# q and k transposed by VectorE in 32x32 blocks, with a new start and a new fill order, in an attention-then-MLP kernel

## The chip, the cores and the metric

One core of one Trainium2 chip. The metric is the device time of one execution in microseconds (us), as the median of several runs. A run is called fast when it lies within 1.5% of the fastest run of the same kernel.

## The reference, cut to what matters

For 8 batches of 8 heads, 576 tokens and 64 values per head, causal attention with a forget gate; its output, laid out as 4608 tokens by 512, goes through a two-layer MLP with an exact GELU.

```python
scores = scale * np.matmul(q, k.transpose(0, 1, 3, 2))
log_f = np.log(np.clip(f, 0.0001, 1.0)); cum = np.cumsum(log_f, axis=-1)
scores = np.where(causal, -1e9, scores + cum[..., :, None] - cum[..., None, :])
attn_out = softmax(scores) @ v                    # B, H, S, D
x = attn_out.transpose(0, 2, 1, 3).reshape(B * S, H * D)
h = x @ w_in                                      # 512 -> 2048
return (0.5 * h * (1 + erf(h / sqrt(2)))) @ w_out # 2048 -> 512
```

q and k are drawn at a scale of 0.1, so a score has a spread of about 0.01 x 8 / 8 = 0.01, and what the softmax does comes almost wholly from the decay.

## The kernel before

Heads go in pairs (four per batch). The score matmuls of this kernel take q and k with their 64 values on partitions; they are loaded with tokens on partitions, transposed by TensorE (PE) into PSUM, and copied by VectorE (DVE) to `qA`, `qB` (one head each, the other half zero) and `kT`:

```python
def transposes(b, i, which):                       # one head pair, q or k
    ps = o_psum.tile([P, 2, JT // 2, PT], BF16, tag="o", name="ps_t")
    for h in range(2):
        for j in range(JT // 2):
            nc.tensor.transpose(ps[:, h, j, :], src[:, 2*i+h, 2*j*D : 2*(j+1)*D], ident_bf[:PT, :PT])
    ...                                            # four copies of 64x288, PSUM -> qA/qB or kT
```

Per pair, `scores` makes four score tiles (PE), their exps (ScalarE, ACT) and causal masks (GpSimd, POOL); `attend` multiplies with v, which GpSimd has weighted by the gate (`weigh_v`). PE's idle moments in attention of batch b are filled with matmuls of `gemm2` of batch b - 1; after attention comes `gemm1`, among whose matmuls the transposes and `weigh_v` of the next batch lie:

```python
for b in range(B):
    fill = gemm2(b - 1) if b else iter(())
    load_qk(b + 2); load_v(b + 2)                  # two buffers each
    for i in range(HP):
        for t in range(4):
            scores(b, i, t)
            ...                                    # attend and normalize of pair i - 1
            take(fill, 2)
    ...                                            # last pair, rest of fill
    for ffb in range(n_ff):
        gemm1(b, ffb)
        if b + 1 < B:
            if ffb % 2 == 1: transposes(b + 1, ffb // 4, (ffb // 2) % 2)
            if ffb % 4 == 2: weigh_v(b + 1, ffb // 4)
```

In the traces every engine runs its instructions in the order in which the program issues them (in e3 below, eight load issues moved within GpSimd's order are worth 41 us). That order carries the whole argument.

The softmax here doesn't subtract the row's maximum and nothing guards it: scores larger than these inputs give would overflow.

## Time and profile before

| | before |
|---|---|
| time, median of 4 runs | 420.51 us (419.28 to 421.01) |
| gemm1 of batch 0 starts | 57.8 us |
| batch period, batches 2 to 6 | 42.8 us |
| gemm1 with transposes / attention, one batch | 15.9 / 26.8 us |
| VectorE per transposed batch | 32 copies of 0.48 us |

The period is the distance between the table loads for Exp on ScalarE, one at each start of attention (119.60 to 333.53 us for five batches). The prediction shows and reads the lines.

### The profile page before, as it was taken

To read this page: it belongs to the slowest core of one execution; us is meant where nothing else is said; L and a number is where in the kernel's file an instruction comes from. 1 tells how busy PE (TensorE), PEld (TensorE's weight loads), DVE (VectorE), ACT (ScalarE), POOL (GpSimd) and SP (SyncE) were. 2 spreads that over 40 slices of the span, in tenths; PEclk is the share of its full clock that TensorE was granted. 3 is DMA by queue.
4 is the path that set the end of the run, shared out by engine and by line. 5 is a ranking of instruction groups with operands and counts; after the bars stand their busy time and mean duration, and the time that the engine had idled before them with its cause. 6 is when DMAs were issued, how large, how long until landed. Compare 5 with 4: busy or idle time off the path is not lost.

```text
span 419.1 us, 7515 instructions
## 1 busy us (share of the span) xinstructions
PE 368.4 (88%) x3045; PEld 207.5 (50%) x3045; DVE 207.2 (49%) x466; ACT 215.0 (51%) x291; POOL 129.5 (31%) x262
## 2 busy tenths in 40 slices
PE   1340879899989998999899989998999999999996
PEld 1220645465546554655465546654664456444442
DVE  6930339534954486448634773468355924102001
ACT  3040736872677267725773577447743675350620
POOL 8408460446034603460247024700470042000000
PEclk9999969999999999999999999999999999999999
DMA  9999985801671166216521643100001000102002
GB/s 156 209 193 196 193 186 125 114 28 54 148 109 31 51 152 93 48 51 152 82 58 52 152 65 74 46 31 2 27 27 51 2 25 28 50 0 77 25 25 77
DMA packets 62738, 34.19 MB, mean 82 GB/s; under 512 B 43184, under 2 KB 57520, under 8 KB 62704
## 3 DMA queue, kind: packets, MB, share of 16 engines
q0 software_dynamic: 15328, 13.63, 20.9%
q1 hardware_dynamic: 47376, 20.08, 18.7%
q8 instruction: 24, 0.39, 0.4%
q14 instruction: 10, 0.08, 0.1%
HBM read 37.90 MB, written 9.44 MB: 113 GB/s over the span
## 4 chain that ended last, share of the span: by engine, by line
PE 77%; ACT 8%; POOL 5%; issue 4%; DVE 4%; ACTq 0%; POOLq 0%
PE ps L277 30%; PE ps L297 26%; PE s L210 7%; PE o L241 7%; ACT e L220 6%; PE ps_t L170 4%; POOL e L222 3%; PE ps_x L265 2%; DVE kT L181 2%; ACT L220 1%; DVE qB L181 1%; DVE qA L181 1%; POOL vw L195 1%; POOL q L98 1%; POOL k L98 1%
## 5 line engine op out<-in xcount | busy, mean ns | idle before, releaser
L289 ACT ACTIVATE g<-ps 128x512 bf16<-128x512 f32 x144 | 86.0, 597 | 125.7 <-PE ps L277 125.7
L297 PE MATMUL ps<-w_out_sb,g 128*128 128x512 bf16 x576 | 146.2, 379 | 0.0
L277 PE MATMUL ps<-xT_sb,w_in_sb 128*128 128x512 bf16 x576 | 136.5, 383 | 0.0
L220 ACT ACTIVATE e<-s 128x1024 bf16<-128x1024 f32 (+2 forms) x128 | 105.7, 862 | 56.2 <-PE s L210 47.6
L222 POOL TENSOR_SCALAR_AFFINE_SELECT e<-e 128x256 bf16<-128x256 bf16 x160 | 62.5, 406 | 114.7 <-ACT e L220 114.3
L277 PEld LDWEIGHTS <-w_in_sb 128*128 128x128 bf16 x576 | 54.0, 99 | 58.2 <-issue 3.5
L241 PE MATMUL o<-vw,e 128*128 128x65 bf16 x960 | 53.9, 196 | 17.7 <-POOL e L222 9.7
L297 PEld LDWEIGHTS <-g 128*128 128x128 bf16 x576 | 49.4, 98 | 37.8
L254 DVE RECIPROCAL r<-o 128x5 f32<-128x5 f32 x64 | 12.5, 195 | 110.5 <-PE o L241 110.5
L210 PE MATMUL s<-qA,kT 128*128 128x384 bf16 (+2 forms) x192 | 54.6, 289 | 11.3 <-ACT e L220 10.3
L181 DVE COPY kT<-ps_t 64x288 bf16<-64x288 bf16 x128 | 61.3, 479 | 2.5 <-PE ps_t L170 0.3
L306 DVE COPY ot<-ps 128x512 f32<-128x512 f32 x36 | 24.7, 687 | 75.7 <-PE ps L297 75.7
L210 PEld LDWEIGHTS <-kT 128*128 128x128 bf16 x384 | 37.2, 100 | 47.1 <-issue 17.2
L241 PEld LDWEIGHTS <-e 128*128 128x128 bf16 x960 | 45.5, 99 | 29.7 <-POOL e L222 11.3
L210 PE MATMUL s<-qB,kT 128*128 128x384 bf16 (+2 forms) x192 | 49.7, 290 | 0.0
L195 POOL TENSOR_TENSOR vw<-v,wT 128x640 bf16<-128x640 f32 x32 | 40.8, 1276 | 15.9 <-issue 13.1
L181 DVE COPY qA<-ps_t 64x288 bf16<-64x288 bf16 x64 | 30.6, 478 | 13.7 <-PE ps_t L170 12.5
L98 POOL DMA_DIRECT2D q<-in_q_dram x11 | 8.4, 766 | 80.3 <-PE ps_t L170 78.7
L255 DVE TENSOR_TENSOR x<-o,r 128x320 bf16<-128x320 f32 x64 | 31.4, 491 | 2.2
L181 DVE COPY qB<-ps_t 64x288 bf16<-64x288 bf16 x64 | 30.7, 480 | 0.9
L170 PE MATMUL ps_t<-ident_bf,q 96*128 96x96 bf16 x192 | 14.6, 216 | 11.6 <-POOL ident_bf masks.py:199 7.2
L170 PEld LDWEIGHTS <-q 96*128 96x128 bf16 x192 | 12.4, 103 | 18.9 <-issue 7.0
(33 smaller groups left out, 117.2 us busy)
## 6 DMA issues: line engine op xcount, KB each, us to landing
out_dram<-ot SPq DMA_DIRECT2D x36, 256.0 KB, 2.0
v<-in_v_dram SPq DMA_DIRECT2D x64, 128.0 KB, 3.1
q<-in_q_dram POOLq DMA_DIRECT2D x7, 576.0 KB, 6.0
k<-in_k_dram POOLq DMA_DIRECT2D x7, 576.0 KB, 8.0
w_in_sb<-in_moe_w_in_dram POOLq DMA_DIRECT2D x4, 512.0 KB, 12.1
v<-in_v_dram SPq DMA_DIRECT2D x8, 256.0 KB, 3.4
w_out_sb<-in_moe_w_out_dram POOLq DMA_DIRECT2D x4, 512.0 KB, 25.7
q<-in_q_dram POOLq DMA_DIRECT2D x4, 144.0 KB, 6.2
```

The source lines that it names most:

```text
L170: nc.tensor.transpose(ps[:, h, j, :], src[:, 2 * i + h, 2 * j * D : 2 * (j + 1) * D], ident_bf[:PT, :PT],)
L181: nc.vector.tensor_copy(rows[:, odd], ps[odd * D : (odd + 1) * D, h].rearrange("d j p -> d p j"),)
L195: nc.gpsimd.tensor_tensor(vw_of[b][:, hs, :, 0:D], v_of[b][:, hs, :, :], w.unsqueeze(3).to_broadcast([P, 2, NBLK, D]), Alu.mult,)
L210: nc.tensor.matmul(st[:, h, c : c + w], kT[i][:, K0[n] : K0[n] + P], qt[:, q0 : q0 + w], start=True, stop=True,)
L220: nc.scalar.activation(et[:, :, 0:c], st[:, :, 0:c], Act.Exp, scale=scale)
L222: nc.gpsimd.affine_select(out=et[:, :, c0 : c0 + P], in_=et[:, :, c0 : c0 + P], compare_op=Alu.is_ge, fill=0.0, base=0, pattern=[[0, 2], [ ...
L241: nc.tensor.matmul(o[:, m, :], e_of[b, i, t][:, h, c : c + P], vw_of[b][:, 2 * i + h, n, :], start=(n == 0), stop=(n == m),)
L255: nc.vector.tensor_tensor(x_of[b, i][:, :, h, :], o[:, :, 0:D], r.unsqueeze(2).to_broadcast([P, NBLK, D]), Alu.mult,)
L277: nc.tensor.matmul(ps, w_in_sb[:, kt, ffb * P : (ffb + 1) * P], xT_sb[:, kt, t0 : t0 + TC], start=(kt == 0), stop=(kt == n_dm - 1),)
L289: nc.scalar.activation(g_of[c][ffb], ps, Act.Gelu)
L297: nc.tensor.matmul(ps, g_of[c][kt][:, ts * P : (ts + 1) * P], w_out_sb[:, kt, :], start=(kt == 0), stop=(kt == n_ff - 1),)
L306: nc.vector.tensor_copy(ot, ps)
```

## The change

It is meant to take the 48 transposes per batch off PE, to start attention of batch 0 earlier, and to give PE filler work while ScalarE starts its exps. q and k of batches 2 to 7 are loaded twice, shifted by half a head, so that blocks of 32 columns can be transposed by VectorE in one instruction; a mask multiplication then separates the heads. The second layout is larger, and the pools of q, k and v shrink from two buffers to one (two of q and k would still have fitted, as e8 shows). The diff, cut to its core:

```diff
-    qk_pool = ctx.enter_context(tc.tile_pool(name="qk", bufs=2))
-    v_pool = ctx.enter_context(tc.tile_pool(name="v", bufs=2))
+    qk_pool = ctx.enter_context(tc.tile_pool(name="qk", bufs=1))
+    v_pool = ctx.enter_context(tc.tile_pool(name="v", bufs=1))
...
+    def load_qk_halves(b):                       # eight loads on GpSimd's queue
...
+        n = JD * D - D // 2
+                nc.gpsimd.dma_start(
+                    dst[:, i, 0:n],
+                    bass.AP(..., ap=[[D // 2, 2], [JD * D, 64], [1, n]]))
...
+    def transposes_dve(b, i, which):
+        src = qk_of[b][which][:, i, :].rearrange("p (j d) -> p j d", j=JD)   # JD = 18
+        dst = kT[i] if which else x_pool.tile([P, S], BF16, tag="qS", name="qS")
+        nc.vector.transpose(
+            dst.rearrange("d (p j) -> d j p", j=JD), src[:, :, 0 : D // 2]
+        )
+        if not which:
+            for h, qt in enumerate((qA[i], qB[i])):
+                nc.vector.tensor_scalar(qt, dst, hmask[:, h : h + 1], None, Alu.mult)
+
+    def transposes(b, i, which):
+        (transposes_pe if b == 1 else transposes_dve)(b, i, which)
...
+    FILL = [[0, 12, 4, 4], [2, 3, 3, 2], [2, 3, 3, 2], [2, 2, 2, 2], [8, 0, 4, 4]]
...                                               # batch 0 and 1: other start, loads reordered
     for b in range(B):
-        load_qk(b + 2)
-        load_v(b + 2)
+            load_v(b + 1)
+            attention(b, gemm2(b - 1), FILL_1 if b == 1 else FILL)
         for ffb in range(n_ff):
             gemm1(b, ffb)
             ...
+        load_qk_halves(b + 2)
```

Two details matter later. The view `"d (p j) -> d j p"` makes the transpose write one element of 2 bytes every 18 elements, that is every 36 bytes. And `load_qk_halves(b + 2)` stands on GpSimd's queue between `weigh_v` of batch b + 1 and the masks of batch b + 1, and can go only when batch b + 1 has been transposed out of the single buffer.

More of the change, by code (lines that the diff above doesn't have):

```diff
@@ L24 @@
 PT = 96
+JD = 18
 STILES = [
@@ L87, with load_qk_tokens @@
     qk_of, v_of = {}, {}
-    def load_qk(b, h0=0, h1=H):
-        if b >= B:
-            return
+    def load_qk_tokens(b, h0=0, h1=H):
         if b not in qk_of:
-            qk_of[b] = (
-                qk_pool.tile([PT, H, JT * D], BF16, tag="q", name=f"q{b}"),
-                qk_pool.tile([PT, H, JT * D], BF16, tag="k", name=f"k{b}"),
-            )
+            qk_of[b] = [
+                qk_pool.tile([P, HP * JD * D], BF16, tag=n, name=f"{n}{b}")[
+                    :PT, : H * JT * D
+                ].rearrange("p (h c) -> p h c", h=H)
+                for n in "qk"
+            ]
         for src, dst in zip((q, k), qk_of[b]):
@@ L101, in load_qk, with load_v @@
             )
-    def load_v(b, h0=0, h1=H):
+    def load_qk_halves(b):
         if b >= B:
             return
+        qk_of[b] = [
+            qk_pool.tile([P, HP * JD * D], BF16, tag=n, name=f"{n}{b}").rearrange(
+                "p (i c) -> p i c", i=HP
+            )
+            for n in "qk"
+        ]
+        n = JD * D - D // 2
+        for src, dst in zip((q, k), qk_of[b]):
+            for i in range(HP):
+                nc.gpsimd.dma_start(
+                    dst[:, i, 0:n],
+                    bass.AP(
+                        tensor=src.tensor,
+                        offset=src.offset + (b * H + 2 * i) * S * D,
+                        ap=[[D // 2, 2], [JD * D, 64], [1, n]],
+                    ),
+                )
+    def load_v(b, h0=0, h1=H, eng=None):
+        if b >= B:
+            return
+        eng = eng or nc.sync
         if b not in v_of:
@@ L108, in load_v @@
         vt = v_of[b]
+        eng.dma_start(
+            vt[:, h0:h1, 4, :], v[b, h0:h1, 448:S].rearrange("h p d -> p h d")
+        )
         for h in range(h0, h1):
-            nc.sync.dma_start(
+            eng.dma_start(
                 vt[:, h, 0:4, :],
@@ L113, in load_v @@
             )
-        nc.sync.dma_start(
-            vt[:, h0:h1, 4, :], v[b, h0:h1, 448:S].rearrange("h p d -> p h d")
-        )
     f_sb = consts.tile([BH, S], FP32)
     nc.sync.dma_start(f_sb, f.rearrange("b h s -> (b h) s"))
-    for i in range(HP):
-        load_qk(0, 2 * i, 2 * i + 2)
-    load_v(0)
+    load_qk_tokens(0, 0, 2)
     ident_bf = consts.tile([P, P], BF16)
@@ L128 @@
     make_identity(nc, ident_fp)
+    for i in range(1, HP):
+        load_qk_tokens(0, 2 * i, 2 * i + 2)
+    v_of[0] = v_pool.tile([P, H, NBLK, D], FP32, tag="v", name="v0")
+    nc.gpsimd.memset(v_of[0][:, :, 4, 0:1], 0.0)
+    load_v(0, 0, 4)
+    load_v(0, 4, 8)
     qA = [consts.tile([P, S], BF16, name=f"qA{i}") for i in range(HP)]
@@ L134 @@
         nc.vector.memset(qB[i][0:D, :], 0.0)
+    hmask = consts.tile([P, 2], FP32)
+    for r in range(4):
+        nc.vector.memset(hmask[32 * r : 32 * (r + 1), 0:1], float(r % 2 == 0))
+        nc.vector.memset(hmask[32 * r : 32 * (r + 1), 1:2], float(r % 2 == 1))
     w_in_sb = consts.tile([P, n_dm, d_ff], BF16)
@@ L141, with load_w_out @@
         nc.gpsimd.dma_start(w_in_sb[:, kt, :], w_in_r[:, kt, :])
-    load_qk(1)
-    load_v(1)
-    for kt in range(0, n_ff, 4):
-        nc.gpsimd.dma_start(w_out_sb[:, kt : kt + 4, :], w_out_r[:, kt : kt + 4, :])
+    def load_w_out():
+        for kt in range(0, n_ff, 4):
+            nc.gpsimd.dma_start(w_out_sb[:, kt : kt + 4, :], w_out_r[:, kt : kt + 4, :])
     wT = consts.tile([P, NBLK, BH], FP32)
@@ L158, with transposes_first, evac, transposes_pe @@
     nc.scalar.activation(wk, cum, Act.Exp, bias=cum[:, S // 2 : S // 2 + 1], scale=-1.0)
-    psw = o_psum.tile([P, NBLK, BH], FP32, tag="o", name="psw")
     xT_sb = consts.tile([P, n_dm, N_tok], BF16)
-    def transposes(b, i, which):
+    def transposes_first(i, which):
+        src = qk_of[0][which]
+        ps = o_psum.tile([P, JT, PT], BF16, tag="o", name="ps_f")
+        for h in range(2):
+            for j in range(JT):
+                nc.tensor.transpose(
+                    ps[h * D : (h + 1) * D, j, :],
+                    src[:, 2 * i + h, j * D : (j + 1) * D],
+                    ident_bf[:PT, :PT],
+                )
+        def evac(eng, dst, r0, r1):
+            op = eng.copy if eng is nc.scalar else eng.tensor_copy
+            op(
+                dst[r0:r1, :].rearrange("d (p j) -> d p j", j=JT),
+                ps[r0:r1].rearrange("d j p -> d p j"),
+            )
+        if which:
+            evac(nc.vector, kT[i], 0, P)
+        else:
+            evac(nc.scalar if i < 2 else nc.vector, qA[i], 0, D)
+            evac(nc.vector, qB[i], D, P)
+    def transposes_pe(b, i, which):
         src = qk_of[b][which]
@@ L184, in transposes @@
                 )
+    def transposes_dve(b, i, which):
[3 more added lines that the diff above has]
+            dst.rearrange("d (p j) -> d j p", j=JD), src[:, :, 0 : D // 2]
+        )
+        if not which:
[3 more added lines that the diff above has]
+        (transposes_pe if b == 1 else transposes_dve)(b, i, which)
     vw_of = {}
@@ L315, in take, with attention @@
                 return
-    for i in range(HP):
-        transposes(0, i, 0)
-        transposes(0, i, 1)
+    FILL = [[0, 12, 4, 4], [2, 3, 3, 2], [2, 3, 3, 2], [2, 2, 2, 2], [8, 0, 4, 4]]
+    FILL_1 = [[0, 0, 0, 0], [0, 0, 0, 0], [2, 3, 3, 4], [4, 4, 4, 4], [12, 0, 6, 6]]
+    def attention(b, fill, counts):
+        for i in range(HP):
+            for t in range(4):
+                scores(b, i, t)
+                if i >= 2 and t == 0:
+                    to_xT(b, i - 2)
+                if i and t == 1:
+                    attend(b, i - 1, 0, (4, 3))
+                elif i and t == 2:
+                    attend(b, i - 1, 0, (2, 1, 0))
+                    normalize(b, i - 1, 0)
+                elif i and t == 3:
+                    attend(b, i - 1, 1, (4, 3, 2, 1, 0))
+                    normalize(b, i - 1, 1)
+                if b == 0:
+                    if i + 1 < HP and t < 2:
+                        transposes_first(i + 1, 1 - t)
+                    if i + 1 < HP and t == 2:
+                        weigh_v(0, i + 1)
+                    if i == 2 and t == 3:
+                        load_qk_tokens(1)
+                    if i == 3 and t == 2:
+                        load_w_out()
+                take(fill, counts[i][t])
+        i = HP - 1
+        take(fill, counts[HP][0])
+        attend(b, i, 0, (4, 3, 2, 1, 0))
+        normalize(b, i, 0)
+        to_xT(b, i - 1)
+        take(fill, counts[HP][1])
+        attend(b, i, 1, (4, 3, 2, 1, 0))
+        normalize(b, i, 1)
+        take(fill, counts[HP][2])
+        to_xT(b, i)
+        take(fill, counts[HP][3])
+        take(fill, 999)
+    transposes_first(0, 1)
+    transposes_first(0, 0)
+    psw = o_psum.tile([P, NBLK, BH], FP32, tag="o", name="psw")
     for n in range(NBLK):
@@ L324 @@
     nc.vector.tensor_copy(wT[D:P, 4, :], psw[D:P, 4, :])
-    for i in range(HP):
-        weigh_v(0, i)
+    weigh_v(0, 0)
     for b in range(B):
-        fill = gemm2(b - 1) if b else iter(())
-        load_qk(b + 2)
-        load_v(b + 2)
-        for i in range(HP):
-            for t in range(4):
-                scores(b, i, t)
-                if i:
-                    if t == 0:
-                        attend(b, i - 1, 0, (4, 3))
-                    elif t == 1:
-                        attend(b, i - 1, 0, (2, 1, 0))
-                        normalize(b, i - 1, 0)
-                    elif t == 2:
-                        attend(b, i - 1, 1, (4, 3))
-                    else:
-                        attend(b, i - 1, 1, (2, 1, 0))
-                        normalize(b, i - 1, 1)
-                if i >= 2 and t == 1:
-                    to_xT(b, i - 2)
-                take(fill, 2)
-        i = HP - 1
-        take(fill, 4)
-        attend(b, i, 0, (4, 3, 2, 1, 0))
-        normalize(b, i, 0)
-        to_xT(b, i - 1)
-        take(fill, 4)
-        attend(b, i, 1, (4, 3, 2, 1, 0))
-        normalize(b, i, 1)
-        take(fill, 8)
-        to_xT(b, i)
-        take(fill, 999)
+        if b == 0:
+            attention(b, iter(()), [[0] * 4] * 5)
+            load_v(1)
+        else:
+            load_v(b + 1)
+            attention(b, gemm2(b - 1), FILL_1 if b == 1 else FILL)
         for ffb in range(n_ff):
```

## The prediction

> **What bounds the kernel now.** I read the busy shares and slices first, then the chain of waits (whole, then its first 60 us and one batch), then the transfers in windows of 2 us, then the engines stage by stage.
>
> ```profile
> PE 368.4 (88%) x3045; PEld 207.5 (50%) x3045; DVE 207.2 (49%) x466; ACT 215.0 (51%) x291; POOL 129.5 (31%) x262
> ...
> PE   1340879899989998999899989998999999999996
> ...
> DMA  9999985801671166216521643100001000102002
> ```
>
> After slice 5 (a slice is 10.5 us) PE is full; before it, PE is nearly empty while the DMA engines are full. So there are two regimes: a start of 58 us bound by transfers, then a PE-bound body. The start, from the chain of the first 60 us:
>
> ```profile
> 23.25 0.48 DVE kT L181
> ...
> 24.45 8.94 issue
> 33.39 0.04 POOL vw L195
> ...
> 40.48 1.84 POOL e L222 x5
> 42.32 0.05 issue
> 42.37 0.51 PE o L241 x6
> ...
> 57.33 0.72 PE ps_x L265 x5
> ```
>
> Until 24 us VectorE empties the transposes of batch 0 (32 copies of 0.48 us); then 8.94 us pass until the first weighting of v (33.4). The page calls this "issue", but the weighting needs v and the DMA engines are full, so I take it as v landing. GpSimd weights four pairs, issues two loads, masks; attention of batch 0 really starts at 42.4 and gemm1 at 57.8. Why v is late, in the transfers of 15 to 17 us and of 65 to 67 us:
>
> ```profile
> q0 software_dynamic: 112, 0.39, 97.1%
> q1 hardware_dynamic: 112, 0.03, 10.1%
> ```
> ```profile
> q1 hardware_dynamic: 1830, 0.45, 100.1%
> ```
>
> Packets of the GpSimd queue (q0) and of the SyncE queue (q1, v) alternate one for one. Beside w_in (4 KB packets) v gets 56 packets per us, beside q and k (768 B) some 190, alone some 915. v of one batch is 5120 packets of 256 B. The body, stage by stage (start, end, busy times):
>
> ```profile
> 145.70:161.60 15.90, 15.90 (x113) 8.23 (x112) 13.90 (x29) 8.99 (x16) 0.81 (x1) 1.00 0.42 100
> 161.60:188.40 26.80, 25.25 (x258) 15.44 (x255) 10.96 (x28) 16.34 (x19) 14.15 (x29) 1.00 0.40 75
> ```
>
> One batch takes 42.7 us: gemm1 15.9 (PE never idle), attention with gemm2 as filler 26.8. In the chain of this batch PE is waited for all the time but at the start of attention:
>
> ```profile
> 162.33 0.76 ACT L220
> 163.09 0.54 issue
> 163.62 1.72 ACT e L220 x2
> ...
> 167.33 0.36 PE o L241 x6
> ```
>
> Between 161.8 and 167.3 us ScalarE loads its table and runs the first exps, and PE has two gemm2 matmuls per step to do: four score tiles 1.4, eight fillers 1.7, the next tile and three attend matmuls 0.5, 3.6 us of work in 5.5. So 1.9 us per batch are idle, and attention holds some 24.8 us of PE work. The tail (359.8 to 419.1 us) has no attention and isn't changed.
>
> **The Trainium skill.** "VectorE: DVE Perf Modes", The three transpose paths: 311 ns for a 128x128 bf16 transpose in 32x32 blocks. That is 128 elements at 0.96 GHz (133 ns) plus 178 ns. The trace has no such transpose, but its copies out of PSUM fit the same sum: 288 elements, 300 ns plus 179 is 479, and 479 ns is measured. I estimate 576/0.96 + 178 = 778 ns for one 128x576 transpose. The same page, The perf-mode tier table, gives bf16 tensor_scalar between SBUF tiles four elements per cycle: 150 ns plus a fixed part, estimate 0.25 to 0.33 us; no such instruction is in the trace. "Trainium Kernel Development and Optimization", Key Constraints: DMAs issued from several queues run on the same 16 engines and interleave. The trace agrees, packet by packet (112 against 112 above).
>
> **The change, part by part.**
>
> *gemm1 of batches 1 to 6.* Gone are 48 PE transposes and 32 VectorE copies per batch. On PE one group of six costs 0.26 us in the chain (161.53), eight are 2.1 us; the tail shows gemm1 without them: 64 matmuls in 13.89 us against 15.9. VectorE: 8 x 0.78 + 8 x 0.3 = 8.6 us in place of 32 x 0.48 = 15.4; both lie beside PE. Only six of the eight gemm1 stages with attention gain: batch 1 keeps PE transposes (done in gemm1 of batch 0), and the last never had any. 6 x 2.1 = **12.6 us**.
>
> *Fill order, attention of batches 2 to 7.* Now 0, 12, 4, 4 fillers in the first pair. Scores 0 and 1 take 0.8 us, twelve fillers 2.6: PE reaches the third tile at 3.4 us after gemm1's end, the first exp ended at 3.1 (164.65 against 161.58). That idle time vanishes. In the rest PE needs 1.39 (scores) + 0.97 (30 attends) + 0.28 + 10 x 0.216 = 4.8 us per pair, ScalarE 3.3, so PE stays full. Near the end there is no filler between the last two attends: the second waits for an o buffer that VectorE frees some 0.9 us after the first, covered by 0.28. I allow 0.7 us. 26.75 to 25.5, 6 x 1.2 = **7.2 us**.
>
> *First batch.* The identity is made after two loads, not eight, so transposes begin at about 5 us. One copy empties 576 elements (0.78) and one pair suffices for scores: first exp at about 10 us instead of 23.7. But v now starts when GpSimd has issued eight loads (1.4 + 8 x 0.63 + 1.1 for identities, about 7.8 us), and w_in right behind it. q and k finish by about 10 us, w_in needs 512 packets at 54 per us, to about 19.7; v has 600 packets by then. The first pair needs 1536: 900 more at 915 per us, plus landing, about 22. Then GpSimd, in order: weighting 1.5, three to four masks 1.6, weighting 1.5, mask 0.4: the first attend at 27 instead of 42.4. Then 4.6 us per pair (five masks 2.0, weighting 1.5, waits for exps 1.1), and in the last two pairs the issue of q1, k1 (1.6) and of w_out (4 x 0.75 = 3.0) stands before a mask: last mask about 42.6, then 3.7 as before (54.1 to 57.8). gemm1 at 46.4 instead of 57.8: **11.4 us**.
>
> *Attention of batch 1.* v1 starts at about 35 us, when v0's tile is free, behind q1, k1 (1536 packets) and w_out (2048): landed at about 57. Weighting 6 us, then eight load issues of 0.6, then masks: first attend near 71, attention having begun near 65. Fillers wait until the third pair. PE has 2.3 us of scores to do in 6 to 7; with ScalarE's pace in the second pair this stage takes about 31 instead of 26.75: **-4.3 us**.
>
> Sum 12.6 + 7.2 + 11.4 - 4.3 = 26.9 us. The span goes from 419.1 to 392.2; the time lies 0.9 above the span, so 393; I say 392.5.
>
> **Rivals.**
> - *Transfers become the bound of the body.* q and k are loaded twice: 8 x 128 packets of 2240 B, 2.29 MB per batch instead of 1.18. At the 180 to 200 GB/s of the cast loads (0.36 MB in 2 us at 79 to 81 us) that is 12 us; v adds 5120/915 = 5.6, the output 1.05 MB some 4. Together 22 of 39 us, and each load has over 25 us. With single buffers, a late load would stop VectorE, then PE. It would cost the 12.6 us or more: about 405 to 410. Unlikely.
> - *VectorE.* With a transpose twice as slow (1.6 us) it works 8 x 1.6 + 2.4 + 11 = 26 of 39 us, and only the first pair is urgent. No loss.
> - *GpSimd.* Eight issues before a mask could hold up each batch by 4.8 us. But VectorE's transposes no longer wait for PE and finish mid-gemm1, so GpSimd issues early. If not, 3 us in each of six batches: about 410.
> - *v is quicker or later than I think in the start.* Were v not starved by w_in it would land near 16 us: 386. If the start saves nothing (the masks and weighting still end at 54 us): 404.
>
> **Range and chances.** The body's 12.6 is near certain, the 7.2 good to 3 us, the start and batch 1 (7.1 net) good to 8. Range 383 to 401. Faster by over 2% (below 411.6) needs under a third of the sum: 0.96. Within 2%: 0.03. Slower: 0.01.
>
> **What would show it.** gemm1 of batch 2 at 13.9 us with PE full; no PE wait on ScalarE at the start of attention from batch 2; batch period about 39.4; transposes near 0.78 us; first weighting near 22 us, gemm1 of batch 0 near 46, attention of batch 1 near 31 with PE idle for some 6. I am wrong if a wait for q, k or v stands on PE's chain in the body, if VectorE's transposes take over 2 us, or if gemm1 of batch 0 starts before 38 or after 54 us.

## The result, and the profile after

The changed kernel took 451.52 us (450.53 to 452.22, 4 runs) against 420.51. The ratio is 1.074, 95% interval 1.0705 to 1.0775: 7% slower, where 392.5 us was foretold. (Ratios here are the mean time of one kernel's fast runs over that of the other's fast runs of the same rounds, so not quite the ratio of the medians quoted.)

The page of the changed kernel: busy time, share and count of PE, then its 40 slices (11.2 us each) and the granted PE clock in tenths:

```profile
PE 367.7 (82%) x2758; PEld 202.5 (45%) x2805; DVE 246.1 (55%) x356; ACT 217.8 (49%) x293; POOL 157.5 (35%) x299
...
PE   3537697999839993999759992999669999999996
...
PEclk9999597999969998799969997899969999999999
```

PE now has a hole in every batch, with a lower clock around it. The start is fuller than before. One batch by stages, gemm1 and then attention (start, end, length; then busy time of PE, of PEld, which is PE's loading of weights, and of DVE, ACT and POOL, each with its count; granted clock, DMA share, GB/s):

```profile
150.60:164.50 13.90, 13.85 (x65) 6.26 (x65) 13.64 (x10) 8.96 (x15) 3.71 (x6) 1.00 0.55 114
164.50:200.10 35.60, 26.59 (x245) 16.36 (x249) 18.44 (x31) 16.64 (x19) 15.22 (x29) 0.86 0.57 89
```

gemm1 lost its 2 us as foretold, but attention grew from 26.8 to 35.6, and VectorE is busy through the whole of gemm1. The groups of instructions say with what (busy us in all, then mean ns of one):

```profile
L249 DVE STREAM_TRANSPOSE qS<-q 128x576 bf16<-128x576 bf16 x24 | 66.9, 2786 | 0.0
L249 DVE STREAM_TRANSPOSE kT<-k 128x576 bf16<-128x576 bf16 x24 | 63.4, 2643 | 0.0
...
L254 DVE TENSOR_SCALAR qA<-qS,hmask 128x576 bf16<-128x576 bf16 x24 | 8.9, 371 | 0.8
```

A transpose takes 2.6 to 2.8 us where 0.78 was estimated. The chain of waits of the same batch (start us, us, what):

```profile
150.79 0.69 DVE ot L379
151.49 2.59 DVE qS L249
154.75 2.56 DVE kT L249
...
168.74 2.49 DVE qS L249
171.51 1.70 POOL q L119 x3
...
174.75 3.13 POOL k L119 x4
177.88 1.85 POOL e L295 x5
179.77 0.51 PE o L314 x6
```

PE isn't in it until 179.8 us. The transposes follow one another on VectorE; GpSimd waits for the last one of q, issues eight loads, masks, and only then may PE attend. The same two waits in the timeline, first GpSimd's, then PE's (start, duration, idle time before and its releaser in brackets):

```profile
171.51 3.19 POOL L119 DMA_DIRECT2D q<-in_q_dram  x4 [17.21 <-DVE qS L249]
```
```profile
179.77 0.51 PE L314 MATMUL o<-vw,e 128*128 128x65 bf16 x6 [8.05 <-POOL e L295]
```

Where the 29.7 us between the two spans (419.1 and 448.8) came from, cut at the Exp table loads:

| stretch | before | after | difference |
|---|---|---|---|
| start to attention of batch 1 | 76.61 | 70.13 | -6.5 |
| to attention of batch 2 | 42.99 | 45.68 | +2.7 |
| to attention of batch 7 (5 batches) | 213.93 | 247.92 | +34.0 |
| to the end | 85.57 | 85.07 | -0.5 |

So the loss is in the five steady batches, 6.8 us each; the period is 49.6 us in place of 42.8. The start, in the transfers from 16 to 18 us (packets, MB, share of 16 engines), shows what it showed before:

```profile
q0 software_dynamic: 111, 0.39, 97.0%
q1 hardware_dynamic: 109, 0.03, 9.9%
```

v gets about one packet of 256 B for each 4 KB packet of w_in, and the first weighting of v began at 24.9 us.

### The profile page after: what moved, and what is told of

Its sections match the earlier page's. It is cut to its first block, busy times and chain, and to the rows that moved or that the text cites. A ratio compares the mean times of both kernels' runs of the same rounds, so it can differ in the third digit from the quotient of the medians.

```text
span 448.8 us, 6952 instructions
## 1 busy us (share of the span) xinstructions
PE 367.7 (82%) x2758; PEld 202.5 (45%) x2805; DVE 246.1 (55%) x356; ACT 217.8 (49%) x293; POOL 157.5 (35%) x299
## 3 DMA queue, kind: packets, MB, share of 16 engines
q0 software_dynamic: 55840, 20.49, 32.7%
## 4 chain that ended last, share of the span: by engine, by line
PE 44%; DVE 30%; POOL 13%; DMA 6%; issue 3%; SPq 3%; ACT 0%; POOLq 0%; ACTq 0%
PE ps L370 22%; DVE qS L249 13%; DVE kT L249 11%; PE o L314 7%; DMA v<-in_v_dram 6%; PE s L283 6%; PE ps L350 6%; POOL k L119 4%; POOL q L119 3%; POOL e L295 3%; SPq L139 3%; PE ps_x L338 2%; DVE qA L254 1%; DVE qB L254 1%; DVE ot L379 1%
## 5 line engine op out<-in xcount | busy, mean ns | idle before, releaser
L370 PE MATMUL ps<-w_out_sb,g 128*128 128x512 bf16 x539 | 143.0, 391 | 2.2 <-issue 0.4
L350 PE MATMUL ps<-xT_sb,w_in_sb 128*128 128x512 bf16 x566 | 128.7, 383 | 0.7 <-issue 0.2
L314 PE MATMUL o<-vw,e 128*128 128x65 bf16 x960 | 51.0, 203 | 61.1 <-POOL e L295 47.5
L249 DVE STREAM_TRANSPOSE qS<-q 128x576 bf16<-128x576 bf16 x24 | 66.9, 2786 | 0.0
L249 DVE STREAM_TRANSPOSE kT<-k 128x576 bf16<-128x576 bf16 x24 | 63.4, 2643 | 0.0
L268 POOL TENSOR_TENSOR vw<-v,wT 128x640 bf16<-128x640 f32 x32 | 40.9, 1279 | 52.4 <-DMA v<-in_v_dram 30.2
L283 PE MATMUL s<-qB,kT 128*128 128x384 bf16 (+2 forms) x192 | 53.3, 307 | 0.1
L119 POOL DMA_DIRECT2D q<-in_q_dram x24 | 19.3, 825 | 89.3 <-DVE qS L249 89.3
L341 DVE COPY xT_sb<-ps_x 128x576 bf16<-128x576 bf16 x32 | 14.6, 455 | 14.4 <-PE ps_x L338 14.4
L119 POOL DMA_DIRECT2D k<-in_k_dram x24 | 18.8, 815 | 0.1
L338 PE MATMUL ps_x<-ident_bf,x 128*128 128x128 bf16 x160 | 15.2, 229 | 2.3 <-DVE x L328 2.2
```

The lines of the kernel that those rows point to most:

```text
L119: nc.gpsimd.dma_start(dst[:, i, 0:n], bass.AP(tensor=src.tensor, offset=src.offset + (b * H + 2 * i) * S * D, ap=[[D // 2, 2], [JD * D, 64 ...
L249: nc.vector.transpose(dst.rearrange("d (p j) -> d j p", j=JD), src[:, :, 0 : D // 2])
L268: nc.gpsimd.tensor_tensor(vw_of[b][:, hs, :, 0:D], v_of[b][:, hs, :, :], w.unsqueeze(3).to_broadcast([P, 2, NBLK, D]), Alu.mult,)
L283: nc.tensor.matmul(st[:, h, c : c + w], kT[i][:, K0[n] : K0[n] + P], qt[:, q0 : q0 + w], start=True, stop=True,)
L314: nc.tensor.matmul(o[:, m, :], e_of[b, i, t][:, h, c : c + P], vw_of[b][:, 2 * i + h, n, :], start=(n == 0), stop=(n == m),)
L350: nc.tensor.matmul(ps, w_in_sb[:, kt, ffb * P : (ffb + 1) * P], xT_sb[:, kt, t0 : t0 + TC], start=(kt == 0), stop=(kt == n_dm - 1),)
```

## The experiments

The theory after the result: the transpose is slow because of how it writes, and it costs time only because GpSimd, in program order, waits for it before it may mask. Ten kernels ran. The first four asked what part of the change costs, why the transpose is slow, and through which wait.

### e1_pe_all: everything but the VectorE transposes

```diff
-        (transposes_pe if b == 1 else transposes_dve)(b, i, which)
+        transposes_pe(b, i, which)
...
-        load_qk_halves(b + 2)
+        if b + 2 < B:
+            load_qk_tokens(b + 2)
```

> All of the change but the VectorE transposes: PE transposes from tokens for every batch from 1 on. Theory (the VectorE transposes, 2.7 us each, and what waits behind them are the whole loss): the 8 us wait of PE for the masks in batches 2 to 7 is gone, batch period about 41.5 us, time 410 to 416 us, so 1 to 2.5% below the kernel before. Rival (the new fill order, the single buffers or the start cost the time): it stays above 430 us.

It took 409.31 us (407.31 to 410.72), ratio 0.9761, interval 0.9707 to 0.9815: faster than the kernel before (the interval lies below 1, though it reaches past a limit of 2%, which makes the formal verdict "unclear"), and a little below the lowest time expected. The period, from Exp loads at 115.07 and 280.73 us, is 41.42 us. So the new start, the fill order and the single buffers together are a gain of 2.4%. The whole loss lies in the VectorE transposes and what hangs on them, the doubled loads included (e2 keeps these and loses nothing by them). Since gemm1 with PE transposes is 15.9 us, attention is 25.5 us with the new fill order.

### e2_dst_contiguous: the transpose writes contiguously

```diff
-            dst.rearrange("d (p j) -> d j p", j=JD), src[:, :, 0 : D // 2]
+            dst.rearrange("d (j p) -> d j p", j=JD), src[:, :, 0 : D // 2]
```

> Wrong result on purpose: the VectorE transpose writes its blocks one after another (unit stride) in place of every 18th column; the same number of elements is read, and everything else is as in the changed kernel. Theory A (the 36-byte stride of the writes makes it slow): the instruction falls from 2.65 us to about 0.8 us, the wait of PE for the masks disappears, the time falls to 388 to 400 us. Theory B (the transpose of 2-byte elements is slow whatever the layout): it stays at 2.5 to 2.8 us and the time within 1% of 451 us.

It took 399.94 us (398.37 to 400.34), ratio 0.9525 (0.949 to 0.956). The groups:

```profile
L249 DVE STREAM_TRANSPOSE kT<-k 128x576 bf16<-128x576 bf16 x24 | 18.5, 770 | 0.0
L249 DVE STREAM_TRANSPOSE qS<-q 128x576 bf16<-128x576 bf16 x24 | 17.8, 742 | 0.0
```

The same transposes of the same number of elements take 0.74 to 0.77 us, and the period, from Exp loads at 115.91 and 273.30 us (four batches), is 39.35 us. The write layout is the cost, and with it the wait of PE for the masks is gone. The result still passed the comparison with the reference, though the tokens are in the wrong order; that fits scores of a spread of 0.01, but means that this comparison doesn't guard the order of q and k. The kernel is an experiment, not a version.

### e4_src_contiguous: the transpose reads contiguously

```diff
-            dst.rearrange("d (p j) -> d j p", j=JD), src[:, :, 0 : D // 2]
+            dst.rearrange("d (p j) -> d j p", j=JD),
+            qk_of[b][which][:, i, 0:S].rearrange("p (j d) -> p j d", j=JD)
```

> Wrong result on purpose: the transpose reads a contiguous run of 576 elements in place of 32 of every 64, and writes with the stride of 18 as in the changed kernel. If the read layout were the cost, the instruction falls to about 0.8 us; by theory A and by theory B it stays at 2.5 to 2.8 us and the time at 450 us.

449.88 us, and transposes of 2.78 and 2.64 us as before. Between these two read layouts there is no difference.

### e3_late_issue: the load issue behind the masks

```diff
-        load_qk_halves(b + 2)
...
+                if b and i == 1 and t == 3:
+                    load_qk_halves(b + 1)
                 take(fill, counts[i][t])
```

> The VectorE transposes stay as slow as they are; only the issue of the q and k loads of the next batch moves from the end of gemm1 into the next attention, behind the masks of its second pair. Theory (the slow transposes cost time only because GpSimd, in order, waits for the single q and k buffers and issues eight loads before it may mask): the 8 us wait of PE for the masks goes, period about 41 to 42 us, time 400 to 412 us. Rival (PE or the normalizing VectorE work itself is held by the transposes, or the load now lands too late): PE waits for VectorE or scores instead, time over 430 us.

It took 410.81 us (409.12 to 411.4), ratio 0.9785 (0.9748 to 0.9821; again "unclear" by the limit of 2%), with transposes as slow as ever (2.79 and 2.65 us). So the place of eight load issues on GpSimd's queue was worth 41 us of time. The period is 41.44 us (Exp loads at 117.44 and 283.20), 2.1 us above that of e2. The end of one batch's chain names the rest (start us, us, what):

```profile
148.32 2.55 DVE kT L249
...
165.48 2.59 DVE kT L249
...
171.96 17.87 DMA k<-in_k_dram
189.83 0.02 issue
189.85 2.65 DVE kT L249
```

From the first k transpose of one batch (148.3 us) to that of the next (189.9 us) it is 41.5 us, the period: 19.8 us of transposes, 3.9 us until the first load of k is issued, and the load of 17.9 us follow one another in the single buffer.

### e8_two_buffers: slow transposes, two buffers for q and k

```diff
-    qk_pool = ctx.enter_context(tc.tile_pool(name="qk", bufs=1))
+    qk_pool = ctx.enter_context(tc.tile_pool(name="qk", bufs=2))
```

> The changed kernel with its slow strided transposes and its load issue where it is, but two buffers for q and k in place of one. Theory (GpSimd is held because the single buffers come free only after the last slow transpose): GpSimd issues the loads during gemm1, the 8 us wait of PE for the masks goes, and the loop of transposes (23 us), issue and load (18 us) that set the 41.4 us period of the late-issue run is open too; period 39.4 to 41 us, time 397 to 408 us. Rival (VectorE itself, 36 us of work per batch and its normalizing behind the transposes, holds PE): over 415 us.

It took 406.79 us (406.1 to 407.34), ratio 0.9668 (0.9624 to 0.9711), and the period is 40.67 us (Exp loads at 116.75 and 279.43). GpSimd's loads, then the one wait of PE that is left near the start of attention, in the timeline:

```profile
146.31 3.27 POOL L119 DMA_DIRECT2D q<-in_q_dram  x4
```
```profile
168.71 0.45 PE L338 MATMUL ps_x<-ident_bf,x 128*128 128x128 bf16 x5 [1.27 <-DVE x L328]
```

GpSimd issues inside gemm1, right behind the weighting. What remains of the slow transposes is 1.3 us per batch in which PE waits for a normalization that stands behind them on VectorE: 40.67 against 39.35. The slow instruction alone costs 1.3 us per batch; with the single buffer and the issue ahead of the masks it costs 10.

### e5_reorder_on_read: contiguous write, tokens ordered by the next read

```diff
-        dst = kT[i] if which else x_pool.tile([P, S], BF16, tag="qS", name="qS")
+        dst = x_pool.tile([P, S], BF16, tag="qS", name="qS")
         nc.vector.transpose(
-            dst.rearrange("d (p j) -> d j p", j=JD), src[:, :, 0 : D // 2]
+            dst.rearrange("d (j p) -> d j p", j=JD), src[:, :, 0 : D // 2]
         )
+        tok = dst.rearrange("d (j p) -> d p j", j=JD)
+        out_of = lambda t: t.rearrange("d (p j) -> d p j", j=JD)
+        if which:
+            nc.vector.tensor_copy(out_of(kT[i]), tok)
         # q: the two masked copies read tok and write out_of(qt)
```

> A right version of the contiguous write: the transpose writes block after block, and the next pass (the two masked copies of q, and a new copy for k) puts the tokens in order by reading with a stride of 64 bytes and writing contiguously. Theory (only the strided write of the transpose is slow; a strided read by an ordinary copy runs near one element per cycle, about 0.6 to 0.8 us for 576 elements): VectorE works about 16 us per batch on it, off PE's path, period 39.4 us, time 397 to 403 us, as in the run with the contiguous write. Rival (any 36- or 64-byte stride is slow on VectorE between SBUF tiles): the new passes take 2 to 3 us each, VectorE becomes the bound, over 440 us.

It took 399.87 us (399.38 to 400.31), ratio 0.9514 (0.9489 to 0.9538), and by its access patterns the tokens are in order. Transposes took 0.77 us, the masked copies 0.72 to 0.78 (0.36 to 0.37 when they read contiguously), the new copy of k 0.76. The period is 39.37 us (117.69 to 275.17). A strided read costs little, and VectorE has the room.

### e6_stride_table: the write stride by itself

Extra VectorE instructions on scratch tiles ahead of the tail of e5, where nothing waits for them. The core of the edit:

```diff
+    for J in (18, 20, 24, 32, 34):                # write stride in elements
+        nc.vector.transpose(sc[:, 0:32*J].rearrange("d (p j) -> d j p", j=J)[:, 0:JD, :], base)
+    for J in (18, 32):
+        nc.vector.tensor_copy(sc[:, 0:32*J].rearrange("d (p j) -> d j p", j=J)[:, 0:JD, :], base)
...                                               # stride 1 of each; 4-byte elements; J = 2 and 6 in pieces
```

> The kernel that reorders on the read, with some thirty extra VectorE instructions on scratch tiles ahead of the tail, to time them: transposes with writes of stride 1, 18, 20, 24, 32 and 34 elements of 2 bytes, of stride 2 and 6 on smaller pieces, of 4-byte elements with stride 1 and 18, and plain copies with the same strided writes. Theory A (2-byte elements written apart are slow in a transpose alone): transposes of 2-byte elements some 2.6 us at strides 18 to 34, 0.75 at stride 1; the plain copies 0.7 to 0.8 at every stride; 4-byte transposes under 1 us at both. Theory B (any write with such a stride is slow): the plain copies take 2.6 us too.

407.03 us with the extra work. The groups: L470 are the strides 18 to 34, L468 stride 1; L474 plain copies at 18 and 32, L477 a plain copy at stride 1; L480 and L479 4-byte elements at stride 18 and 1; L484 pieces at stride 6 (192 elements) and 2 (64 elements):

```profile
L470 DVE STREAM_TRANSPOSE sc<-xT_sb 128x576 bf16<-128x576 bf16 x5 | 13.6, 2718 | 0.2
L474 DVE COPY sc<-xT_sb 128x576 bf16<-128x576 bf16 x2 | 2.8, 1413 | 0.1
L484 DVE STREAM_TRANSPOSE sc<-xT_sb 128x192 bf16<-128x192 bf16 x3 | 2.0, 867 | 0.0
L480 DVE STREAM_TRANSPOSE sf<-cumf 128x576 f32<-128x576 f32 x1 | 1.3, 1259 | 0.0
L484 DVE STREAM_TRANSPOSE sc<-xT_sb 128x64 bf16<-128x64 bf16 x9 | 1.2, 209 | 0.0
L479 DVE STREAM_TRANSPOSE sf<-cumf 128x576 f32<-128x576 f32 x1 | 0.8, 772 | 0.0
L468 DVE STREAM_TRANSPOSE sc<-xT_sb 128x576 bf16<-128x576 bf16 x1 | 0.7, 719 | 0.0
L477 DVE COPY sc<-xT_sb 128x576 bf16<-128x576 bf16 x1 | 0.3, 311 | 0.0
```

Neither theory was quite right. From stride 18 to 34 the time hardly depends on the stride (2.65 to 2.82 us). At stride 6 it is already 867/192 = 4.5 ns per element, about the 2718/576 = 4.7 of the larger strides (each with the fixed part of an instruction in it); at stride 2 (64 elements in 209 ns) no such cost shows. Plain copies pay as well, 1.4 us in place of 0.31, half of what the transpose pays; and 4-byte elements pay less, 1.26 against 0.77. So at the strides tried a plain copy and a transpose of 4-byte elements are slow to write too, and a transpose of 2-byte elements is the worst case of those tried. Which part of the hardware does it, the runs don't show.

### e7a_w_in_behind_v and e7b_w_out_behind_v1: the order of loads in the start

Both start from e5.

```diff
 # e7a
-    for kt in range(n_dm):                        # ahead of everything on v
-        nc.gpsimd.dma_start(w_in_sb[:, kt, :], w_in_r[:, kt, :])
...
     weigh_v(0, 0)
+    load_w_in()
 # e7b, on top of it
-                    if i == 3 and t == 2:
-                        load_w_out()
...
                     weigh_v(b + 1, ffb // 4)
+                    if b == 0 and ffb // 4 == 1:
+                        load_w_out()
```

> The reordering kernel with w_in issued behind the first weighting of v in place of ahead of it. Theory (in the start v is starved by the 4 KB packets of w_in, packet for packet): v lands near 14 to 16 us in place of 24.8, attention of batch 0 and gemm1 of batch 0 come some 8 us earlier (43 in place of 51.2), the time falls by 4 to 8 us against the reordering kernel. Rival (the start is bound by GpSimd and ScalarE, or w_in now comes late): gemm1 of batch 0 starts after 48 us and the time stays within 2 us.

> The same, and w_out issued behind the second weighting of v of batch 1 in place of within attention of batch 0. Theory (v of batch 1 is starved by w_out in the same way and holds GpSimd, and so the masks of batch 1): v of batch 1 lands 8 to 12 us sooner, the idle time of PE in the first pairs of batch 1 shrinks, another 3 to 6 us. Rival (w_out then comes too late for gemm2 of batch 0): PE waits for w_out, no gain or a loss.

e7a took 391.35 us (389.68 to 392.16), ratio 0.932 (0.9292 to 0.9348): 8.5 us under e5, at the far end of what was expected. The first weighting of v, in e5 and then in e7a (the timeline of GpSimd):

```profile
24.79 1.28 POOL L274 TENSOR_TENSOR vw<-v,wT 128x640 bf16<-128x640 f32 x1 [14.88 <-DMA v<-in_v_dram]
```
```profile
14.45 1.28 POOL L275 TENSOR_TENSOR vw<-v,wT 128x640 bf16<-128x640 f32 x1 [6.65 <-DVE qB L212]
```

The weighting starts 10 us sooner, in this trace no longer held by v last, and gemm1 of batch 0 starts at 43.2 us in place of 51.4. The start was bound by v behind w_in.

e7b took 388.94 us (387.83 to 389.5), ratio 0.9251 (0.9223 to 0.9278): 2.4 us under e7a, less than expected. gemm1 of batch 0 starts 4.2 us sooner, at 38.9 us; most of that fits the 3.0 us issue of w_out no longer standing before the last mask of batch 0. But the Exp load of batch 1 comes only 2.0 us sooner (59.1 us), for within gemm1 PE now waits 1.6 us for k of batch 1. The last weighting of batch 1 starts at 52.4 us instead of 58.4, yet counted from that Exp load the attends didn't come sooner: PE's wait for the masks ended 7.6 us after it (66.7 us), in e7a 6.9 us (68.0 us). GpSimd's last load issue for batch 2 now waited 1.55 us for w_out, and the masks stand behind it.

### e9_batch1_loads_late: the loads of batch 2 behind masks of batch 1

```diff
-        load_qk_halves(b + 2)
+        if b:
+            load_qk_halves(b + 2)
...
+                if b == 1 and i == 1 and t == 3:
+                    load_qk_halves(2)
                 take(fill, counts[i][t])
```

> The kernel with w_in behind v0 and w_out behind v1, and the loads of batch 2 issued behind the masks of the second pair of batch 1 in place of ahead of all masks of batch 1 (there the last of the eight issues waited for w_out, 1.55 us). Theory (in batch 1 GpSimd's load issues hold the masks until 66.7 us): the first attend of batch 1 comes 6 to 9 us after gemm1 of batch 0 becomes 4 to 6, the time falls by 3 to 5 us to 384 to 386. Rival (ScalarE's exps and the fill order of batch 1 bound this stage, or the load of batch 2 then comes late): within 1.5 us of 388.9.

It took 387.36 us (385.83 to 388.26), ratio 0.9204 (0.9163 to 0.9245), the lowest of all; its interval overlaps that of e7b, so the two aren't told apart. The expected 3 to 5 us didn't come. The masks of batch 1 start 5 us sooner (59.6 us), but the stretch from the Exp load of batch 1 to that of batch 2 is as long as in e7b (57.24 to 104.05 against 59.13 to 106.00, 46.8 and 46.9 us): the load issues, 67.0 to 73.4 us, now stand before the masks of the third pair. PE then waits 1.3 us for a mask there (at 75.3 us). What bounds batch 1 after that was not tried.

## Why the prediction was wrong, step by step

**The step that failed** is the estimate "576/0.96 + 178 = 778 ns for one 128x576 transpose", and with it two sentences: that with transposes twice as slow there is "No loss", and that "VectorE's transposes no longer wait for PE and finish mid-gemm1, so GpSimd issues early". The 778 ns hold for a contiguous write: 719 to 770 ns measured in e2, e5 and e6. The kernel writes with a stride of 36 bytes, and that instruction takes 2640 to 2790. I took the element rate from a table and from copies whose innermost write stride is 4 bytes, and never asked about the write side of the new one, though the diff shows it. The prediction named the sign, transposes of over 2 us, but not what would bring them about. On VectorE's own side "No loss" is off by 1.3 us per batch (e8); it failed through GpSimd, whose early issue the single buffers tied to the end of the transposes.

**How 2 us per instruction became 10 us per batch.** Eight transposes and eight masked copies take 23 us where gemm1 takes 13.9. The single buffers come free only then, about 7 us into attention; GpSimd waits for that, issues eight loads in 6.3 us (4.8 were foretold), masks, and PE's attend waits 8.05 us in the timeline. The prediction's GpSimd rival had this wait in it, and put it at 3 us per batch "If not". The three experiments that take away one link each agree: the fast write (period 39.35 us), the second buffer (40.67), the later issue (41.44), against 49.6. The PE clock, granted at 0.86 in that attention stage and at 1.00 in gemm1, adds something after each wait. No run isolates it, but PE is busy for 26.6 us in that stage and for 24.7 us in the same stage of e2 (154.6 to 180.1 us, clock 1.00); so an estimate is some 1.9 of the 10 us, beside the 8.05 of the wait.

**gemm1, 12.6 us:** right. 13.9 us per batch with the transposes gone, beside 15.9, so 12.0 over six batches.

**Fill order, 7.2 us:** right. e1 leaves attention at 41.42 - 15.9 = 25.5 us, the number foretold; e2 and e5 have the period of 39.4 us foretold, to 0.1.

**First batch, 11.4 us:** right in its mechanism, wrong in size. v came behind w_in, packet for packet, but the first weighting was at 24.9 us, not 22, and from there to gemm1 it took 26.9 us rather than 24.4: gemm1 started at 51.8 instead of 46.4, a gain of 6.0 us. e7a confirms the mechanism: with w_in behind v the first weighting starts 10 us sooner.

**Batch 1, minus 4.3 us:** right in size, in part by luck. Attention of batch 1 lasts from 70.1 to 101.3 us in the changed kernel, 31.2 us; 31 was foretold. GpSimd did wait for v there, but v came later than the foretold 57 us (the last pair could be weighted only at 66.9), while three of the four weightings were already done by then, and attention began at 70.1, not 65.

Put together, e2, which is the change with the transpose that I had in mind, has a span of 396.7 us; the sum foretold 392.2: 4.5 us more. Its gemm1 of batch 0 starts at 51.2 us, 4.8 later than foretold, so the first batch explains it. (The time was put 0.9 us above the span; the profiled run of the kernel before lies 1.95 above its own, 421.05 against 419.1, a slip of one us.) The rest of the miss, 448.8 - 396.7 = 52 us, is the strided write and what waited for it.

**The load of q and k** was also mis-sized. The 1024 packets of 2240 B per batch are in the trace as foretold. But of the 55840 packets of that queue 44064 have 4 bytes, and in one batch (171 to 196 us) they are 7296 beside the 1024. Shared among 16 engines, the large ones took 13.2 us and the small ones 4.7 us, where 12 us in all were foretold; one load took 16 us at the median from issue to landing. By the packets' times, only about two rows are in flight while one load is under way alone (173.1 to 174 us) and about 18 with all eight; the two loads of a batch in the old layout keep about 21 in flight (e1). So a load of the new layout moves two rows at a time. No run shows why (its source pattern begins with a dimension of two), nor what the small packets are for: a load in the old layout has 16 of them, one of these has 912. The load stayed hidden but for e3, where it closed a loop.

## What to carry to other kernels

Before an instruction's cost is taken from a table or from a sibling, compare the write stride too; where tokens must be interleaved, write contiguously and let the next pass read with the stride. An instruction off the critical path still decides when its buffer comes free: on an engine that runs in order, a load that waits for a single buffer holds every later piece of work there, here the masks, so give it a second buffer or issue it behind the urgent work. And two queues that alternate packet for packet starve the one with small packets: issue the large-packet load behind the small one that is needed first (8.5 us here).

## What the Trainium skill lacked or had wrong

- "VectorE: DVE Perf Modes", The three transpose paths: the section gives one time per size and says nothing of the write stride. (A general warning is elsewhere, in "SBUF — State Buffer" under cachelines: accesses that each cross to a new 16-byte line pay a penalty, with no figure for VectorE. The write strides tried fit it, but the read with a stride of 64 bytes below doesn't, and no run shows the reason.) The runs show 0.72 to 0.77 us for 128x576 bf16 written contiguously (its 311 ns for 128x128 scale to that) and 2.65 to 2.82 us at strides of 36 to 68 bytes; 4.5 ns per element already at 12 bytes, no such cost at 4.
- The same page, Walkthrough: the 8-slice pipeline in each mode, has the slowest mode give one result per cycle and work with "weird strides". A copy of 576 bf16 elements between SBUF tiles, written with a stride of 36 or 64 bytes, took 1.40 to 1.43 us, over two cycles per element at 0.96 GHz; read with a stride of 64 bytes and written contiguously it took 0.76, about what the page says.
- The same page, The perf-mode tier table: the masked bf16 multiply with contiguous access took 0.36 to 0.37 us, a little over the 0.25 to 0.33 estimated from it.
- "DMA: Bandwidth & Descriptors", Queues, rings and completion order: it says that an engine goes round between the queues packet by packet, with some 9 to 17 descriptors to a packet. The equal counts of the trace fit the turns (111 against 109 in 2 us; a packet of the trace is one row). What the page does not say is what follows for a queue of 256 B packets beside one of 4 KB packets: 56 packets per us in place of 915.
